# VectorE instead of GpSimd in the first network's weight decode and in the attention of blocks 1 to 8

## The chip, the cores and the metric

The kernel runs on one core of a Trainium2 chip. Its engines work side by side, each through its own queue in order: PE (TensorE, matmuls; PEld is its weight loads), DVE (VectorE), ACT (ScalarE), POOL (GpSimd) and SP (SyncE, which here issues most DMAs). The metric is the time of one execution on the device, in microseconds (us).

## The reference

Attention without a product of q and k, then two networks on its result:

```python
q_s = exp(q - max(q, axis=-1));  q_s /= sum(q_s, axis=-1) + 1e-09
k_s = exp(k - max(k, axis=2));   k_s /= sum(k_s, axis=2) + 1e-09   # along the sequence
x = einsum(q_s, einsum(k_s, v))                                    # 4608 tokens x 512
x = relu(x @ w_in) ** 2 @ w_out                                    # 512 -> 2048 -> 512
xn = x / sqrt(mean(x * x) + 1e-06) * rms_g
out = (silu(xn @ w_gate) * (xn @ w_val)) @ w_out2                  # 512 -> 1536 -> 512
```

q, k and v are 8 batches of 8 heads of 576 positions of 64 numbers. All is fp32.

## The kernel before

The tokens are worked off in 9 blocks of 512. For each block j, attention gives x in four parts, one for each pair of heads (hp), and the first network makes h = x @ w_in in 16 column tiles c, squares relu(h) to g and adds g @ w_out into four PSUM banks (`acc`). Such a pair of steps (j, c) is a unit: `p1_A` makes g of unit c, `p1_B` adds it two units later. The result of a block goes to DRAM after four copies out of PSUM (`e`, two by DVE, two by ACT). The second network runs behind about 955 us, over the same blocks, and is not touched.

Every fp32 matmul is made of three passes (`mm3`, L98): each operand is split into a high part (a rounding copy by ACT) and a low part (the difference, by DVE in `split`, L78). So each g costs one ACT copy and one DVE subtraction, and so do qT, kvd (k^T v of a head pair) and x.

The weights come as 64-bit floats and are decoded on the chip, tile by tile. A tile of weights is a key: i0 to i15 are column tiles of w_in, o0 to o15 row tiles of w_out; the second network has its own keys. `tick` moves the decode on by one key: `d_load` (512 KB by SP into one of three `raw` buffers), `d_words` (s, the high word scaled, L216, POOL; n, the low word, L224, ACT), `d_float` (three steps on DVE, L235, L243 and L247, that put the float together in one of two `t` buffers), `d_split` (high part by ACT, L251, low part by POOL, L252). The first network's keys are decoded while block 0 uses them, until about 140 us; to fill PE, h of block 1 is made along with them from i9 on. Keys of the second network are decoded from about 255 to 860 us, most of them in bursts up to 580 us (L295 makes sums of tiles on POOL, L252 splits them as `so`), and are written to DRAM.

Attention of block j + 1 goes along with block j's units. `A_STEPS` gives each head pair's steps with their unit: maxima of q and k (L471, L407, L410, DVE), subtraction of q's maxima (`a_qsub`, L477, POOL), `a_ktr` (PE transposes k's maxima, DVE reduces them, mc, L421, and spreads them, mcb, L423), `a_kb` (PE transposes them back into the PSUM tile `ps_kb`; ACT copies that to `mb`, L434), exp of q (ACT), `a_ksub` (two pieces, L445, POOL), the sum over q (`a_qsum`, L485 to L487, DVE), exp of k (`a_kexp`, ACT), scaling of q (`a_qn`, L494, POOL), k^T v (PE, normalized by DVE, L542 to L546), transposition of q (PE), x (PE). All PSUM tiles of attention (ps_kt, ps_kb, ps_kv, ps_q, ps_x) take turns in two buffers. Block 0's attention runs ahead of everything, with k's maxima subtracted straight from PSUM by DVE and q scaled by DVE.

The order on each engine is set by a scheduler, except for what `held` keeps in program order: such an instruction stays behind all that was written before it on its engine.

## Time and profile before

| | |
|---|---|
| time, median of 3 runs | 1826.89 us (1826.87 to 1830.08) |
| the profiled execution's own time | 1822.36 us |
| its span in the trace | 1820.6 us |
| PE busy | 1751.3 us (96%) |
| DVE busy | 1062.1 us (58%) |
| ACT busy | 750.9 us (41%) |
| POOL busy | 351.9 us (19%) |

POOL's share is a mean over the whole span; behind 860 us POOL does nothing. PE is near fully busy everywhere else than in the first 140 us and in some places between 280 and 560 us. So the stretches are to be read apart, by the windows view, and in each of them what PE waits for.

### The profile page before, as it was taken

To read this page: it belongs to the slowest core of one execution; us is meant where nothing else is said; L and a number is where in the kernel's file an instruction comes from. 1 tells how busy PE (TensorE), PEld (TensorE's weight loads), DVE (VectorE), ACT (ScalarE), POOL (GpSimd) and SP (SyncE) were. 2 spreads that over 40 slices of the span, in tenths; PEclk is the share of its full clock that TensorE was granted. 3 is DMA by queue.
4 is the path that set the end of the run, shared out by engine and by line. 5 is a ranking of instruction groups with operands and counts; after the bars stand their busy time and mean duration, and the time that the engine had idled before them with its cause. 6 is when DMAs were issued, how large, how long until landed. Compare 5 with 4: busy or idle time off the path is not lost.

```text
span 1820.6 us, 27274 instructions
## 1 busy us (share of the span) xinstructions
PE 1751.3 (96%) x10346; PEld 1520.1 (83%) x10346; DVE 1062.1 (58%) x1792; ACT 750.9 (41%) x1371; POOL 351.9 (19%) x349
## 2 busy tenths in 40 slices
PE   5789998999988999999999999999999999999998
PEld 3568886888767888888889999999999999999997
DVE  7875467374674534322245757676767675757544
ACT  4455435454554444444444232333333333333322
POOL 4666226154664412120000000000000000000000
PEclk9899999999989999999999999999999999999999
DMA  6787657688996755565757676767676767676673
GB/s 176 226 262 269 210 190 257 203 270 270 330 320 229 233 177 190 173 224 180 292 190 251 226 258 211 261 212 256 215 259 215 257 210 258 215 244 231 212 236 131
DMA packets 173634, 420.19 MB, mean 231 GB/s; under 512 B 57408, under 2 KB 74816, under 8 KB 172352
## 3 DMA queue, kind: packets, MB, share of 16 engines
q1 hardware_dynamic: 162272, 377.55, 63.4%
q10 hardware_dynamic: 11232, 40.90, 5.9%
q8 instruction: 83, 1.36, 0.3%
q14 instruction: 47, 0.39, 0.1%
HBM read 358.62 MB, written 59.77 MB: 230 GB/s over the span
## 4 chain that ended last, share of the span: by engine, by line
PE 75%; DMA 4%; DVE 2%; POOL 2%; issue 1%; ACT 1%; POOLq 0%; ACTq 0%; SPq 0%; DVEq 0%
PE acc L98 30%; PE ps_h L98 14%; PE ps_y L738 8%; PE ps_x L738 8%; PE ps_v L738 8%; PE ps_w L738 4%; DMA wd_s<-so 1%; DMA wd_a<-so 1%; POOL so L252 1%; PE ps_x L98 1%; PE ps_kv L526 1%; DMA wd_u<-so 1%; DVE t L243 1%; DVE t L235 0%; PE ps_q L508 0%
## 5 line engine op out<-in xcount | busy, mean ns | idle before, releaser
L98 PE MATMUL ps_h<-x,ws 128*128 128x512 f32 x1296 | 325.0, 401 | 6.7 <-POOL ws L252 5.9
L78 DVE TENSOR_TENSOR g<-r,g 128x512 fp32r<-128x512 f32 x252 | 191.3, 761 | 232.7 <-ACT g L77 230.7
L98 PE MATMUL acc<-g,ws 128*128 128x512 f32 x1296 | 315.8, 392 | 11.2 <-DVE e L620 5.6
L98 PEld LDWEIGHTS acc<-g,ws 128*128 128x128 f32 x1296 | 243.8, 189 | 64.6 <-POOL ws L252 7.3
L98 PEld LDWEIGHTS ps_h<-x,ws 128*128 128x128 f32 x1296 | 242.4, 192 | 59.3 <-POOL ws L252 7.9
L98 PE MATMUL acc<-ws,g 128*128 128x512 f32 x1080 | 265.7, 392 | 0.4 <-DVE g L78 0.4
L98 PEld LDWEIGHTS acc<-ws,g 128*128 128x128 f32 x1080 | 195.8, 189 | 37.9 <-DVE g L78 1.8
L77 ACT ACTIVATE g<-r 128x512 fp32r<-128x512 f32 x252 | 157.6, 626 | 44.5 <-DVE r L722 30.9
L720 ACT ACTIVATE sg<-c 128x256 f32<-128x256 f32 x108 | 56.5, 524 | 273.0 <-DVE c L753 223.0
L589 ACT ACTIVATE r<-ps_h 128x512 f32<-128x512 f32 x144 | 85.5, 594 | 202.7 <-PE ps_h L98 194.4
L738 PE MATMUL ps_x<-x,ws 128*128 128x256 f32 x972 | 129.5, 283 | 0.0
L738 PEld LDWEIGHTS ps_x<-x,ws 128*128 128x128 f32 x972 | 124.7, 191 | 3.0
L738 PE MATMUL ps_v<-x,ws 128*128 128x256 f32 x864 | 115.1, 283 | 0.0
L738 PEld LDWEIGHTS ps_v<-x,ws 128*128 128x128 f32 x864 | 111.0, 191 | 2.8
L98 PE MATMUL ps_h<-x,w 128*128 128x512 f32 x432 | 110.2, 405 | 0.0
L98 PE MATMUL acc<-g,w 128*128 128x512 f32 x432 | 108.1, 399 | 1.8 <-POOL w L252 1.5
L738 PE MATMUL ps_y<-x,ws 128*128 128x256 f32 x756 | 101.7, 284 | 0.0
L98 PEld LDWEIGHTS acc<-g,w 128*128 128x128 f32 x432 | 82.7, 193 | 19.8 <-POOL w L252 1.9
L753 DVE TENSOR_TENSOR c<-ps_v,u 128x512 f32<-128x512 f32 x54 | 37.4, 692 | 105.1 <-PE ps_v L738 105.1
L738 PEld LDWEIGHTS ps_y<-x,ws 128*128 128x128 f32 x756 | 95.1, 192 | 2.3 <-DVE sa L661 2.3
L98 PEld LDWEIGHTS ps_h<-x,w 128*128 128x128 f32 x432 | 81.7, 194 | 17.5
L590 ACT ACTIVATE r<-r 128x512 f32<-128x512 f32 x144 | 89.9, 628 | 3.0
(114 smaller groups left out, 2490.5 us busy)
## 6 DMA issues: line engine op xcount, KB each, us to landing
ws<-wd_s SPq DMA_DIRECT2D x135, 512.0 KB, 4.3
ws<-wd_a SPq DMA_DIRECT2D x117, 512.0 KB, 4.5
ws<-wd_o SPq DMA_DIRECT2D x96, 512.0 KB, 4.1
ws<-wd_i SPq DMA_DIRECT2D x90, 512.0 KB, 4.2
ws<-wd_u SPq DMA_DIRECT2D x90, 512.0 KB, 4.2
raw<-in_w_out SPq DMA_DIRECT2D x28, 512.0 KB, 4.9
raw<-in_w_gv SPq DMA_DIRECT2D x24, 512.0 KB, 6.1
wd_s<-so ACTq DMA_DIRECT2D x24, 512.0 KB, 5.5
```

Of the source, the lines that this page charges most:

```text
L77: held(j, nc.scalar.activation(out=dst[:, 0], in_=src, func=AF.Copy))
L78: nc.vector.tensor_tensor(out=dst[:, 1], in0=src, in1=dst[:, 0].bitcast(F32), op=ALU.subtract)
L98: ins = nc.tensor.matmul(ps, lhsT(a), rhs(b), start=first and n == 0, stop=last and n == 2)
L243: nc.vector.scalar_tensor_tensor(out=t, in0=sb, scalar=0x80000000, in1=t, op0=ALU.bitwise_and, op1=ALU.bitwise_or)
L252: eng.tensor_tensor(out=t[:, 1], in0=f, in1=t[:, 0].bitcast(F32), op=ALU.subtract)
L526: ins = nc.tensor.matmul(ps[h * D : (h + 1) * D, 0 : D + 1], ke[0:m, c, h, :], vt[0:m, c, h, :], start=c == 0, stop=c == SF,)
L589: nc.scalar.activation(out=r, in_=ps, func=AF.Relu)
L590: nc.scalar.activation(out=r, in_=r, func=AF.Square)
L720: nc.scalar.activation(out=r, in_=h[:, :, 0], func=AF.Sigmoid)
L738: nc.tensor.matmul(ps[:, g * HF : (g + 1) * HF], w[:, wa, (2 * g + kk) * P : (2 * g + kk + 1) * P], x[:, xa, kk, :], start=first and g == ...
L753: nc.vector.tensor_tensor(out=sv(name), in0=in0, in1=in1, op=ALU.add)
```

## The change

Four things change. The scaled high word s of the first network's keys is made by DVE for keys i and by ACT for keys o (the second network's stays on POOL), and the low parts of all 32 of these keys by DVE. k's maxima stay in the PSUM tile `ps_kb`: ACT's copy `mb` is gone, and DVE subtracts from PSUM, in the same step as the transposition (`a_kbs`, one unit earlier); exp of k is one unit earlier too. q's subtraction and scaling are DVE's in all blocks from 1 on. And the subtractions, the sum over q and the scaling are no longer held in program order. POOL keeps a memset of vt's column of ones and the second network's decode.

```diff
--- before.py
+++ after.py
@@ -213,14 +213,14 @@
         r = raws.pop(key).bitcast(U32).rearrange("p (n two) -> p n two", two=2)
         s = pools["d"].tile([P, 512], F32, tag="s", name="s", bufs=2)
         n = pools["d"].tile([P, 512], I32, tag="n", name="n", bufs=2)
-        nc.gpsimd.tensor_scalar(
-            out=s,
-            in0=r[:, :, 1].bitcast(F32),
-            scalar1=2.0**-112,
-            scalar2=0.0,
-            op0=ALU.mult,
-            op1=ALU.add,
-        )
+        hi = r[:, :, 1].bitcast(F32)
+        if key[0] == "o":
+            nc.scalar.activation(out=s, in_=hi, func=AF.Copy, scale=2.0**-112)
+        else:
+            eng = nc.vector if key[0] == "i" else nc.gpsimd
+            eng.tensor_scalar(
+                out=s, in0=hi, scalar1=2.0**-112, scalar2=0.0, op0=ALU.mult, op1=ALU.add
+            )
         nc.scalar.activation(out=n, in_=r[:, :, 0], func=AF.Copy, scale=2.0**-29)
         words[key] = s, n
 
@@ -265,7 +265,7 @@
 
     def d_split(key):
         t = slot_tile(key) if key in res1 else ring_tile()
-        w_split(t, floats.pop(key), nc.gpsimd)
+        w_split(t, floats.pop(key), nc.vector)
         if key not in res1:
             send(key, t, 2)
         wt[key] = t
@@ -428,27 +428,25 @@
             return
         ps = a_ps(j, hp, "ps_kb")
         held(j, nc.tensor.transpose(ps[:, 0:P], mcs.pop((j, hp)), ident))
-        mb = ps
-        if j > 0:
-            mb = pools["a"].tile([P, P], F32, tag="mb", name="mb", bufs=1)
-            nc.scalar.activation(out=mb, in_=ps[:, 0:P], func=AF.Copy)
-        mcs[j, hp] = mb
+        mcs[j, hp] = ps
 
     def a_ksub(j, hp):
         if j >= B:
             return
         kt = kts[j, hp]
         mx = mcs.pop((j, hp))[:, 0:P].rearrange("p (h d) -> p h d", h=2).unsqueeze(2)
-        eng = nc.gpsimd if j > 0 else nc.vector
         for rows, cs in k_parts:
             n = cs.stop - cs.start
-            ins = eng.tensor_tensor(
+            nc.vector.tensor_tensor(
                 out=kt[rows, :, cs, :],
                 in0=kt[rows, :, cs, :],
                 in1=mx[rows].to_broadcast([rows.stop, 2, n, D]),
                 op=ALU.subtract,
             )
-            held(j, ins)
+
+    def a_kbs(j, hp):
+        a_kb(j, hp)
+        a_ksub(j, hp)
 
     k_parts = ((slice(0, P), slice(0, SF)), (slice(0, SR), slice(SF, SF + 1)))
 
@@ -474,7 +472,8 @@
     def a_qsub(j, hp):
         qv = q_heads(j, hp)
         qm = qms.pop((j, hp)).unsqueeze(2).to_broadcast([P, 2 * NG, D])
-        held(j, nc.gpsimd.tensor_tensor(out=qv, in0=qv, in1=qm, op=ALU.subtract))
+        eng = nc.vector if j > 0 else nc.gpsimd
+        eng.tensor_tensor(out=qv, in0=qv, in1=qm, op=ALU.subtract)
 
     def a_qexp(j, hp):
         qv = q_heads(j, hp)
@@ -482,7 +481,7 @@
 
     def a_qsum(j, hp):
         qs = pools["a"].tile([P, 2 * NG], F32, tag="qs", name="qs")
-        held(j, nc.vector.reduce_sum(out=qs, in_=q_heads(j, hp), axis=AX.X))
+        nc.vector.reduce_sum(out=qs, in_=q_heads(j, hp), axis=AX.X)
         nc.vector.tensor_scalar_add(out=qs, in0=qs, scalar1=1e-9)
         nc.vector.reciprocal(out=qs, in_=qs)
         qms[j, hp] = qs
@@ -491,13 +490,12 @@
         qt = qts.pop((j, hp))
         rs = qms.pop((j, hp)).rearrange("p (h c) -> p h c", h=2).unsqueeze(3)
         qn = pools["a"].tile([P, NG, 2, D], F32, tag="qn", name="qn", bufs=2)
-        ins = (nc.gpsimd if j > 0 else nc.vector).tensor_tensor(
+        nc.vector.tensor_tensor(
             out=qn.rearrange("p c h d -> p h c d"),
             in0=qt,
             in1=rs.to_broadcast([P, 2, NG, D]),
             op=ALU.mult,
         )
-        held(j, ins)
         qns[j, hp] = qn
 
     def a_qT(j, hp):
@@ -830,7 +828,7 @@
 
 
     A_STEPS = ((-3, a_loadk), (-2, a_loadq), (0, a_qmax), (0, a_kmax), (1, a_qsub), (1, a_ktr))
-    A_STEPS += ((2, a_kb), (2, a_qexp), (3, a_ksub), (3, a_qsum), (3, a_loadv), (4, a_kexp))
+    A_STEPS += ((2, a_kbs), (2, a_qexp), (3, a_qsum), (3, a_loadv), (3, a_kexp))
     A_STEPS += ((4, a_qn), (5, a_kvn), (6, a_qT), (7, a_x))
     A_STARTS = {1: (-6, -4, -2, 0), 2: (-6, -3, 0, 3)}
     todo = {}
```

DVE behind block 0's x, in block 1's attention (t and s are buffers of the decode, w_649 is key i1's tile, g the first split of h). Before:

```order
L471 TENSOR_REDUCE qm<-qt 128x8
L487 RECIPROCAL qs<-qs 128x8
L423 COPY mcb<-mc 128x128
L78 TENSOR_TENSOR g<-r,g 128x512
L247 ISA t<-t,n 128x1024
L542 TENSOR_SCALAR rk<-ps_kv 128x1
L235 TENSOR_SCALAR t<-s 128x512
L543 RECIPROCAL rk<-rk 128x1
L243 SCALAR_TENSOR_TENSOR t<-s,t 128x512
L546 SCALAR_TENSOR_TENSOR kvf<-ps_kv,rk,mask 128x128
L247 ISA t<-t,n 128x1024
```

Now:

```order
L541 RECIPROCAL rk<-rk 128x1
L485 TENSOR_SCALAR qs<-qs 128x8
L410 TENSOR_TENSOR mk<-mk,kt 64x128
L544 SCALAR_TENSOR_TENSOR kvf<-ps_kv,rk,mask 128x128
L486 RECIPROCAL qs<-qs 128x8
L421 TENSOR_REDUCE mc<-ps_kt 128x1
L476 TENSOR_TENSOR qt<-qt,qm 128x512
L78 TENSOR_TENSOR kvd_0_87<-kvf,kvd_0_87 128x128
L423 COPY mcb<-mc 128x128
L78 TENSOR_TENSOR g<-r,g 128x512
L252 TENSOR_TENSOR w_649<-t,w_649 128x512
```

The low part of i1 was POOL's; it now stands on DVE behind the attention of block 1's first head pairs.

DVE in the later part of the first decode, about two keys (ws are weight tiles). Before:

```order
L78 TENSOR_TENSOR qT<-ps_q,qT 128x512
L243 SCALAR_TENSOR_TENSOR t<-s,t 128x512
L247 ISA t<-t,n 128x1024
L542 TENSOR_SCALAR rk<-ps_kv 128x1
L235 TENSOR_SCALAR t<-s 128x512
L543 RECIPROCAL rk<-rk 128x1
L243 SCALAR_TENSOR_TENSOR t<-s,t 128x512
L546 SCALAR_TENSOR_TENSOR kvf<-ps_kv,rk,mask 128x128
L78 TENSOR_TENSOR g<-r,g 128x512
L247 ISA t<-t,n 128x1024
```

Now:

```order
L252 TENSOR_TENSOR ws<-t,ws 128x512
L235 TENSOR_SCALAR t<-s 128x512
L221 TENSOR_SCALAR s<-raw 128x512
L243 SCALAR_TENSOR_TENSOR t<-s,t 128x512
L235 TENSOR_SCALAR t<-s 128x512
L247 ISA t<-t,n 128x1024
L243 SCALAR_TENSOR_TENSOR t<-s,t 128x512
L493 TENSOR_TENSOR qn<-qt,qs 128x2x4x64
L252 TENSOR_TENSOR ws<-t,ws 128x512
L247 ISA t<-t,n 128x1024
L235 TENSOR_SCALAR t<-s 128x512
```

The scaling s and the low parts ws have come in between the steps of the floats, and so has the scaling of q.

DVE at the end of block 1, from the g split to the first of its two e copies. Before:

```order
L78 TENSOR_TENSOR g<-r,g 128x512
L235 TENSOR_SCALAR t_3665<-s 128x512
L243 SCALAR_TENSOR_TENSOR t_3665<-s,t_3665 128x512
L247 ISA t_3665<-t_3665,n 128x1024
L235 TENSOR_SCALAR t_3745<-s 128x512
L243 SCALAR_TENSOR_TENSOR t_3745<-s,t_3745 128x512
L235 TENSOR_SCALAR t_3882<-s 128x512
L620 COPY e<-acc_2111 128x512
```

Now:

```order
L440 TENSOR_TENSOR kt<-kt,ps_kb 128x2x256
L78 TENSOR_TENSOR g<-r,g 128x512
L440 TENSOR_TENSOR kt<-kt,ps_kb 64x2x64
L484 TENSOR_REDUCE qs<-qt 128x8
L235 TENSOR_SCALAR t_3642<-s 128x512
L485 TENSOR_SCALAR qs<-qs 128x8
L235 TENSOR_SCALAR t_3719<-s 128x512
L486 RECIPROCAL qs<-qs 128x8
L243 SCALAR_TENSOR_TENSOR t_3642<-s,t_3642 128x512
L493 TENSOR_TENSOR qn<-qt,qs 128x2x4x64
L618 COPY e<-acc_2099 128x512
```

The subtraction of k's maxima, the sum over q and the scaling of q stand here now, and fewer steps of the decode.

DVE in the units around 513 us, up to the reduction mc. Before:

```order
L487 RECIPROCAL qs<-qs 128x8
L247 ISA t_6068<-t_6068,n 128x1024
L235 TENSOR_SCALAR t_6198<-s 128x512
L243 SCALAR_TENSOR_TENSOR t_6198<-s,t_6198 128x512
L78 TENSOR_TENSOR g<-r,g 128x512
L247 ISA t_6198<-t_6198,n 128x1024
L421 TENSOR_REDUCE mc<-ps_kt 128x1
L423 COPY mcb<-mc 128x128
```

Now:

```order
L247 ISA t_6025<-t_6025,n 128x1024
L235 TENSOR_SCALAR t_6152<-s 128x512
L243 SCALAR_TENSOR_TENSOR t_6152<-s,t_6152 128x512
L407 TENSOR_REDUCE mk<-kt 128x128
L78 TENSOR_TENSOR g<-r,g 128x512
L421 TENSOR_REDUCE mc<-ps_kt 128x1
L410 TENSOR_TENSOR mk<-mk,kt 64x128
L423 COPY mcb<-mc 128x128
```

The reduction mc, which frees a PSUM buffer, moved from behind the last step of a key to the place right behind the g split.

## Rows read from the trace of the kernel before

**Rows 1.** Windows by stage: each engine busy (instructions), PEclk, DMA share, GB/s.

```profile
36.50:140.00 103.50, 82.21 (x386) 60.49 (x385) 84.50 (x137) 53.66 (x105) 65.09 (x60) 0.91 0.70 224
...
250.00:580.00 330.00, 309.02 (x1560) 250.15 (x1559) 208.45 (x326) 165.28 (x310) 172.32 (x159) 0.96 0.81 269
580.00:955.00 375.00, 375.00 (x1824) 308.89 (x1823) 131.18 (x230) 165.28 (x290) 56.93 (x58) 1.00 0.61 205
```

**Rows 2.** PE's waits, 36.5 to 140 us: total, times, longest.

```profile
PE ps_h L98 <- POOL ws L252: 5.9, 4, 2.1
```

**Rows 3.** DVE's groups, 36.5 to 140 us: shapes, count, busy, mean ns, idle.

```profile
L243 DVE SCALAR_TENSOR_TENSOR t<-s,t 128x512 uint32<-128x512 uint32 x20 | 19.9, 995 | 0.5
L247 DVE CUSTOM_DVE_ANT_0 t<-t,n 128x1024 uint16<-128x1024 uint16 x21 | 17.2, 817 | 1.2
L235 DVE TENSOR_SCALAR t<-s 128x512 uint32<-128x512 uint32 x20 | 11.1, 553 | 13.2 <-POOL ws L252 10.5 <-POOL w L252 2.4 <-POOL s L216 0.3
...
L78 DVE TENSOR_TENSOR kvd<-kvf,kvd 128x128 fp32r<-128x128 f32 x5 | 5.2, 1033 | 0.1
...
L423 DVE COPY mcb<-mc 128x128 f32<-128x128 f32 x4 | 2.4, 611 | 0.0
```

**Rows 4.** DVE's timeline around 101 us: start, duration.

```profile
101.39 0.43 DVE L235 TENSOR_SCALAR t<-s 128x512 uint32<-128x512 uint32 x1 [1.56 <-POOL ws L252]
101.85 0.69 DVE L243 SCALAR_TENSOR_TENSOR t<-s,t 128x512 uint32<-128x512 uint32 x1
102.69 0.69 DVE L247 CUSTOM_DVE_ANT_0 t<-t,n 128x1024 uint16<-128x1024 uint16 x1
```

**Rows 5.** DVE's groups up to 36.5 us (block 0's attention).

```profile
L494 DVE TENSOR_TENSOR qn<-qt,qs 128x512 f32<-128x512 f32 x4 | 2.8, 701 | 1.2 <-PE ps_q L508 1.2
...
L445 DVE TENSOR_TENSOR kt<-kt,ps_kb 128x512 f32<-128x512 f32 x4 | 2.7, 674 | 0.0
...
L78 DVE TENSOR_TENSOR kvd<-kvf,kvd 128x128 fp32r<-128x128 f32 x3 | 0.8, 279 | 0.0
```

**Rows 6.** DVE's groups from 250 to 580 us.

```profile
L78 DVE TENSOR_TENSOR g<-r,g 128x512 fp32r<-128x512 f32 x50 | 48.0, 964 | 49.1 <-ACT g L77 49.1
L247 DVE CUSTOM_DVE_ANT_0 t<-t,n 128x1024 uint16<-128x1024 uint16 x34 | 33.9, 1006 | 1.2 <-ACT n L224 0.3
L243 DVE SCALAR_TENSOR_TENSOR t<-s,t 128x512 uint32<-128x512 uint32 x34 | 31.8, 939 | 0.6
L235 DVE TENSOR_SCALAR t<-s 128x512 uint32<-128x512 uint32 x34 | 22.8, 679 | 14.6 <-POOL so L252 12.6 <-POOL s L216 1.9
```

**Rows 7.** POOL's groups from 250 to 580 us.

```profile
L445 POOL TENSOR_TENSOR kt<-kt,mb 128x512 f32<-128x512 f32 x12 | 18.0, 1497 | 2.5 <-ACT mb L434 2.5
L494 POOL TENSOR_TENSOR qn<-qt,qs 128x512 f32<-128x512 f32 x12 | 14.2, 1183 | 47.1 <-DVE qs L487 47.1
L477 POOL TENSOR_TENSOR qt<-qt,qm 128x512 f32<-128x512 f32 x12 | 12.5, 1043 | 9.4 <-DMA kt<-in_k 4.8 <-DVE qm L471 4.6
```

**Rows 8.** PE's waits from 250 to 580 us.

```profile
PE ps_x L98 <- DVE qT L78: 6.3, 3, 2.9
PE acc L98 <- DVE e L620: 5.6, 1, 5.6
PE ps_kv L526 <- issue: 5.3, 1, 5.3
```

**Rows 9.** DVE's timeline around 280 and 513 us.

```profile
276.26 1.76 DVE L78 TENSOR_TENSOR g<-r,g 128x512 fp32r<-128x512 f32 x1
...
285.41 0.68 DVE L620 COPY e<-acc 128x512 f32<-128x512 f32 x1
...
512.67 0.86 DVE L235 TENSOR_SCALAR t<-s 128x512 uint32<-128x512 uint32 x1 [3.19 <-POOL so L252]
```

**Rows 10.** DVE's g splits from 860 to 955 us (POOL silent).

```profile
L78 DVE TENSOR_TENSOR g<-r,g 128x512 fp32r<-128x512 f32 x17 | 11.8, 692 | 47.2 <-ACT g L77 47.2
```

## The prediction

> **What bounds the kernel now.** I read the busy time by stage first. Between 36.5 and 140 us, the decode of the first network's weights, PE is busy for 82.2 of 103.5 us; between 250 and 580 us, the decode of the second network's, for 309.0 of 330; from 580 to 955 us it never stands still [rows 1]. The second network, behind 955 us, the change does not touch. So only two stretches can pay: 21.3 us of idle PE in the first and 21.0 us in the second. Each also has matmuls at a clock under full: granted 0.91 and 0.96 on average [rows 1].
>
> In the first stretch, PE's waits name one thing: the low half of a weight tile from POOL (L252). The row shown is one of three like it, 13.0 us together [rows 2]. DVE's groups tell why POOL is late: L235, the first step of a key's decode on DVE, sat idle for 13.2 us because its buffer was still being read by POOL [rows 3]. It is a loop: three steps on DVE, one on ACT, one on POOL, then DVE again. PE is a follower there.
>
> In the second stretch the waits that end PE's gaps point at DVE: an e copy 5.6 us, qT 6.3 us, and 5.3 us at ps_kv [rows 8]; that last one is booked as issue, but PE starts again right behind DVE's mc step, which frees a PSUM buffer, so I take it as DVE's too. DVE is 63% busy there on average (208.5 of 330, rows 1), and much more in bursts.
>
> **The change, part by part.** The first decode (36.5 to 140 us). POOL leaves the loop; the question is what DVE then needs for the same work. DVE was busy 84.5 us [rows 1]. Part of that is stretching beside POOL. Alone, L235 takes 0.43, L243 0.69, L247 0.69 [rows 4] and kvd 0.28 [rows 5]; in the stretch they take 0.553, 0.995, 0.817 and 1.033 [rows 3]. The small copy mcb takes 0.611 [rows 3] and stands for three kinds of small steps that are stretched; alone it is 0.21 (a row not shown). With POOL silent, 20 x 0.305 + 21 x 0.127 + 20 x 0.123 + 4 x 0.40 + 5 x 0.754 = 16.6 us go, and 67.9 are left.
>
> Then the additions. Scaling s for the 10 of 20 keys that begin with i: no row shows it on DVE; the nearest is L235, the same kind and shape, so 10 x 0.43 = 4.3. The low halves: 20 on DVE; the nearest row is a split of the same shape and type, 0.692 [rows 10], so 13.8. Attention for four head pairs: subtracting k's maxima, 0.674 from PSUM [rows 5] and 0.267 for the small second piece (its row is not shown), and q's subtraction and scaling, 0.701 each [rows 5], so 4 x 2.34 = 9.4. Together 27.5. The groups of [rows 3] and those not shown add to 91.9 us where the window counts 84.5, because neighbours overlap: 0.054 us for each of 137 instructions. For the 46 new ones that is 2.5 us back. 67.9 + 27.5 - 2.5 = 92.9 us.
>
> So DVE alone cannot finish in less than 92.9 us what took 103.5: at most 10.6 us to gain. It will not be fully busy. Of its 19.0 us of idle time, the 13.2 in front of L235 go [rows 3], the other 5.8 (for PE, for ACT) I keep. 98.7 us, a gain of 4.8. New on DVE is a wait inside a key: L252 needs ACT's high half. The order mostly puts the next key's steps between, so I add nothing; where L252 stands directly behind its key's L247, about half a microsecond is at stake. One place is worse: the low half of key i1 now stands behind block 1's whole first burst of attention, so PE has only key i0 and attention until then. The count above contains that burst, because the stretch is bounded by DVE's sum and PE has 21 us of slack. The ends: -10.6, and +3 if 3 us of round trips of that burst and of L252 appear on top of a DVE that gets none of its stretching back in the steps that pull most (kvd and mcb, 5.4 us). I take -4.8, near the middle.
>
> ACT gains ten scalings of keys o, about 0.66 each by its like-shaped step n, and loses four copies of maxima; it was busy for 53.7 of 103.5 us [rows 1], its idle time covers it. Loads: the same bytes in 98.7 instead of 103.5 us are 235 instead of 224 GB/s, and the second decode moved 269 [rows 1]. Both at nothing.
>
> The second decode (250 to 580 us). POOL keeps this network's decode and loses attention: 18.0 + 14.2 + 12.5 = 44.7 of its 172.3 us [rows 7, 1]. DVE gets 12 head pairs x 2.34 = 28.1 us. What it gets back: L247, L243, L235 and g take 1.006, 0.939, 0.679 and 0.964 here [rows 6], against 0.69, 0.69, 0.43 [rows 4] and 0.692 [rows 10]; that is 34 x 0.316 + 34 x 0.249 + 34 x 0.249 + 50 x 0.272 = 41.3 us of stretching beside 172.3 us of POOL, 0.24 each. For 44.7 us: 10.7. Net +17.4, DVE at 226 of 330, 68%.
>
> PE does not pay an average but its gaps, so I go through those with the order. The gap at 280 us (5.6): the e copy starts at 285.41, 7.4 us behind the end of the g split that started at 276.26 [rows 9]; in the new order only 3.5 us of DVE work stand between them, with 0.67 more ahead of the split: 3 us earlier at best. I take 2, since two of the steps between wait for POOL's s. The gap at 513 us (5.3): DVE sat 3.19 us until 512.67 for a POOL split [rows 9] that stood behind one scaling and one subtraction of q; these leave POOL and cost DVE 1.4 itself. Also mc now directly follows the g split. I take 2. The gap at 461 us (2.6 of the 6.3 for qT) has the same DVE rows ahead of it in both orders, decode alone: nothing. The gap at 555 us has more rows ahead, and fewer by POOL beside them: nothing. Against this, 12 new portions of 2.34 us, of which I let one show: +2. Sum -2. The ends: -10 (PE's three waits of rows 8 are 17.2 us; little over half goes) and +11.7 (five portions show).
>
> Blocks behind 580 us: PE has no gap there and DVE is busy 131 of 375 us [rows 1]; four head pairs are 9.4 us per block of about 94. k's maxima now hold a PSUM buffer until DVE has subtracted, not until ACT has copied; the buffer is wanted again two units later. The earlier kexp and the missing holds move work that PE does not wait for. Nothing, with 2 us either way.
>
> **Sum.** -4.8 - 2 = -6.8. The profiled execution took 1822.36 us and would take 1815.6. The median of the three runs, 1826.89, lies 4.5 us above it; I carry the same difference over: **1820 us**.
>
> **Rivals.** First, DVE too late in the second decode, **slower**. Place: the queue of DVE from 250 to 580 us, where ksub, both halves of it, two sums and a scaling now stand between g splits in the same units as the decode. A g split of the same shape costs 0.964 there against 0.692 alone, so 24 new subtractions and scalings with both inputs in SBUF would add 24 x 0.27 = 6.5 us to the 17.4. It decides where PE reaches ps_q, ps_x or a g tile before DVE has worked off a portion: if that is so for half of 12 head pairs, 6 x 2.34 = 14 us, less the 4.8: +9, about 1836. For it: DVE releases nearly all of PE's waits here. Against it: the average of 68%, and the two gaps above that shrink.
> The Trainium skill, "SBUF — State Buffer", section "Who interferes with whom", says that VectorE and GpSimd share a port pair as an exclusive lock, which an instruction of VectorE with two SBUF inputs also needs against a GpSimd instruction that reads SBUF. By that rule the 24 are exposed and the subtraction of k's maxima from PSUM is not; the trace agrees as far as L243, with two SBUF inputs, goes (0.995 beside POOL, 0.69 alone).
>
> Second, **no change**: DVE, now the bound of the first decode, idles 10 us and not 5.8 (the burst ahead of i1's low half, L252 behind ACT), and the second decode gives nothing back: 0 to -3, about 1825.
>
> Third, **a larger gain**: the first decode comes near DVE's sum (-9) and the second loses half of the two gaps that I only shortened by 2, with the slow clock behind them (-7): -16, about 1811.
>
> **Chances.** Forecast (-3.7 to -12) 0.48, larger gain 0.12, no change 0.18, slower 0.22. 0.2% is 3.65 us, about what a measurement of this kernel can tell from no change. Faster 0.60, same 0.18, slower 0.22. The range 1809 to 1834 leaves out some 0.06 below and 0.12 above; it spans -18 to +7, that is the low ends of both terms nearly together, and the slower case without its tail.
>
> **What would show it.** Right: between 36.5 and about 135 us DVE busy over 90%, POOL nearly empty, L243 near 0.69 us, PE's last wait for a weight tile some 5 us earlier, and its waits there on DVE L252; around 280 and 513 us shorter gaps. Wrong: DVE with over 10 us of idle time in the first stretch; new waits of PE for DVE between 290 and 580 us that sum to over 5 us; any gap of PE behind 580 us.

## The result

The changed kernel takes 1809.26 us, median of 4 runs (1806.02 to 1810.44); the kernel before, beside it, 1828.49 (1826.87 to 1835.79). The ratio is 0.9884, with a 95% interval of 0.9854 to 0.9915. The profiled execution of after took 1806.02 us with a span of 1804.2, against 1822.36 and 1820.6.

So it became faster by 19 us, in the medians, and by 16.4 in the two traces; 6.8 had been forecast. The time lies at the very lower end of the range, and it is the rival "a larger gain" (-9 and -7, to which 0.12 was given) that came true.

The stages of after, by the windows view (columns as in [rows 1]):

```profile
36.50:140.00 103.50, 89.82 (x434) 68.40 (x434) 97.65 (x205) 66.07 (x124) 0.60 (x4) 0.92 0.77 246
250.00:580.00 330.00, 312.67 (x1590) 254.08 (x1589) 219.68 (x379) 168.49 (x309) 121.80 (x110) 0.97 0.81 270
580.00:955.00 375.00, 375.00 (x1850) 310.08 (x1849) 141.39 (x259) 164.13 (x281) 18.81 (x19) 1.00 0.63 212
```

Against [rows 1]: between 36.5 and 140 us POOL has gone from 65.1 us to 0.6, DVE from 84.5 to 97.7, PE from 82.2 to 89.8. Between 250 and 580 us PE has 312.7 instead of 309.0 us of work done, at a clock of 0.97 instead of 0.96, with POOL at 121.8 instead of 172.3. Behind 580 us PE is as full as it was. (The first decode does not end at 140 us, as the description of the kernel before has it: its last low half ends at 184.8 us, with the change at 171.0. What ends by 140 us are PE's waits for it.)

How PE's waits changed in the first decode, and how DVE's groups did (36.5 to 126.5 us, where the same 20 keys are through; to be read against [rows 2, 3]):

```profile
PE ps_kb L430 <- DVE mcb L423: 4.9, 4, 2.7
PE ps_kt L419 <- DVE mk L410: 2.9, 2, 2.2
...
PE ps_h L98 <- DVE ws L252: 1.2, 2, 0.9
```

```profile
L247 DVE CUSTOM_DVE_ANT_0 t<-t,n 128x1024 uint16<-128x1024 uint16 x20 | 13.5, 678 | 0.1
L243 DVE SCALAR_TENSOR_TENSOR t<-s,t 128x512 uint32<-128x512 uint32 x20 | 13.4, 677 | 0.0
L252 DVE TENSOR_TENSOR ws<-t,ws 128x512 fp32r<-128x512 f32 x15 | 10.1, 674 | 1.5 <-ACT ws L251 1.5
L235 DVE TENSOR_SCALAR t<-s 128x512 uint32<-128x512 uint32 x20 | 8.1, 412 | 0.0
...
L78 DVE TENSOR_TENSOR g<-r,g 128x512 fp32r<-128x512 f32 x9 | 6.1, 674 | 0.0
...
L78 DVE TENSOR_TENSOR kvd<-kvf,kvd 128x128 fp32r<-128x128 f32 x5 | 1.4, 279 | 1.3 <-ACT kvd L77 1.3
...
L423 DVE COPY mcb<-mc 128x128 f32<-128x128 f32 x4 | 0.8, 203 | 0.0
```

L243 is back at 0.677 us (0.995 before), kvd at 0.279 (1.033), mcb at 0.203 (0.611). L235 no longer waits at all (13.2 us before). PE's waits for POOL are gone; its largest waits are for the maxima of block 1's attention, between 41 and 54 us.

A measure that goes through the whole study: the start of DVE's first e copy at the end of a block, which needs all matmuls of that block. "Between" is the time from block 0's to block 4's.

| kernel | block 0 | block 4 | between | median of the runs |
|---|---|---|---|---|
| before | 195.2 | 596.6 | 401.4 | 1826.9 to 1828.8 in five measurements |
| changed | 184.2 | 579.1 | 394.9 | 1809.3 |
| changed, once more | 184.1 | 578.0 | 393.9 | 1809.0 |
| decode alone (e1) | 185.6 | 590.8 | 405.2 | 1818.0 |
| attention alone (e2) | 192.9 | 582.9 | 390.0 | 1816.1 |
| POOL's attention from block 3 (e3) | 185.4 | 593.4 | 408.0 | 1821.8 |
| POOL's q from block 3 (e20) | 184.5 | 585.1 | 400.6 | 1813.7 |
| holds back (e4) | 186.8 | 584.3 | 397.5 | 1815.4 |
| ACT's copy of the maxima back (e10) | 187.0 | 585.1 | 398.1 | 1815.8 |
| five so buffers (e11) | 183.9 | 587.5 | 403.6 | 1815.8 |
| extra work on DVE (e5) | 185.6 | 575.0 | 389.4 | 1808.1 |
| extra work on POOL (e6) | 196.1 | 589.7 | 393.6 | 1819.3 |
| all s on ACT (e7) | 183.1 | 581.8 | 398.7 | 1808.7 |
| i1 on POOL (e8) | 181.7 | 580.6 | 398.9 | 1808.6 |
| block 2's maxima held (e16) | 182.3 | 574.5 | 392.2 | 1804.0 |
| the same, once more | 182.6 | 584.0 | 401.4 | 1807.6 |
| held, and i1 on POOL (e19) | 178.5 | 575.9 | 397.4 | 1804.2 |
| before, three t buffers (e9) | 195.1 | 604.7 | 409.6 | 1830.8 |

The two pairs of repeats say how such a table is to be read: block 0's end repeats to 0.3 us, the time between to no better than 1 us in one pair and 9 us in the other. So the first column tells of a single edit, the third only with the medians beside it. Nor do the columns add up to the medians: behind block 4's e copy the traces still differ by 5.6 us (1224.0 to 1229.6).

What varies between the blocks can be read from the windows view over just that stretch, here for the kernel before, the changed kernel, and the two executions with block 2's maxima held:

```profile
195.20:596.60 401.40, 380.42 (x1939) 308.98 (x1938) 238.09 (x382) 196.39 (x369) 183.72 (x174) 0.97 0.76 251
```

```profile
184.20:579.10 394.90, 377.57 (x1938) 307.48 (x1937) 252.74 (x446) 193.53 (x353) 123.88 (x114) 0.98 0.77 255
```

```profile
182.30:574.50 392.20, 375.06 (x1939) 304.75 (x1938) 258.17 (x450) 193.83 (x354) 124.83 (x114) 0.99 0.77 258
```

```profile
182.60:584.00 401.40, 380.35 (x1939) 309.33 (x1938) 257.95 (x449) 194.21 (x354) 125.21 (x114) 0.97 0.76 251
```

PE works off the same matmuls each time. The last two differ by 9.2 us: 3.9 are idle time of PE (17.1 against 21.1), and 5.3 are the same matmuls taking longer, at a granted clock of 0.97 instead of 0.99.

### The profile page after: what moved, and what is told of

Its sections match the earlier page's. It is cut to its first block, busy times and chain, and to the rows that moved or that the text cites. A ratio compares the mean times of both kernels' runs of the same rounds, so it can differ in the third digit from the quotient of the medians.

```text
span 1804.2 us, 27227 instructions
## 1 busy us (share of the span) xinstructions
PE 1746.3 (97%) x10346; PEld 1518.4 (84%) x10346; DVE 1100.0 (61%) x1960; ACT 754.6 (42%) x1359; POOL 154.6 (9%) x165
## 4 chain that ended last, share of the span: by engine, by line
PE 83%; DVE 8%; DMA 5%; issue 1%; ACT 1%; POOL 1%; SPq 0%; POOLq 0%; DVEq 0%; ACTq 0%
PE acc L98 33%; PE ps_h L98 18%; PE ps_y L736 8%; PE ps_x L736 8%; PE ps_v L736 8%; PE ps_w L736 4%; DMA wd_s<-so 2%; DVE t L243 1%; PE ps_x L98 1%; DVE t L247 1%; DMA wd_a<-so 1%; PE ps_kv L524 1%; DVE t L235 1%; PE ps_q L506 1%; DVE g L78 1%
## 5 line engine op out<-in xcount | busy, mean ns | idle before, releaser
L78 DVE TENSOR_TENSOR g<-r,g 128x512 fp32r<-128x512 f32 x252 | 182.8, 726 | 212.6 <-ACT g L77 210.3
```

Source lines behind the costliest of these rows:

```text
L78: nc.vector.tensor_tensor(out=dst[:, 1], in0=src, in1=dst[:, 0].bitcast(F32), op=ALU.subtract)
```

## The experiments

**The two halves apart.** One kernel with the decode's part of the diff alone, one with the attention's part alone.

```diff
 # e1_decode_only: the kernel before, d_words and d_split as in the change
 # e2_attention_only: the changed kernel, d_words and d_split as before
```

> The kernel before with one part of the change: the first network's decode off POOL (s by DVE for keys i and by ACT for keys o, all low parts by DVE); attention stays on POOL, with its holds. Theory A (the gain of the first decode comes from taking POOL out of the decode's loop, DVE is then the bound; the gain of the second decode comes from the attention's move): the first e copy of block 0 starts 8 to 10 us earlier than in the kernel before (195.2 us there, 184.2 with the whole change), nothing changes between block 0 and block 4, in all 8 to 10 us less. Theory B (POOL was late because attention stood in its queue; the decode alone would have been quick enough there): block 0 gains 3 us or less.

> The kernel with the whole change but the decode, which stays on POOL as before: only attention is moved. Theory A: the loop over POOL stays, L235 still waits for L252, and block 0's first e copy comes 3 to 5 us earlier at most (about 191 us); between block 0's and block 4's e copies 6 us are gained as with the whole change; in all 9 to 11 us less. Theory B: block 0 gains 8 to 11 us here already, in all 14 to 17 us less.

Measured: decode alone 1818.04 us, ratio 0.9945 (0.9927 to 0.9963); attention alone 1816.14, ratio 0.9933 (0.9908 to 0.9957). Theory A stands for the places: the decode's part gives 9.6 of the 11 us at block 0's end, the attention's part 2.3, and of what comes behind block 0 the attention's part gives all. By the medians, both beside the same runs of the kernel before, the parts are 9.8 and 11.7 us; together they gave 18 to 19 in other measurements, somewhat less than their sum. What was too small is the attention's part behind block 0: 9 us by the medians, where 2 had been put down, and 11.4 in the trace of e2, where 6 had been expected.

**Two buffers, or POOL's work?** L235 waited 13.2 us for a buffer [rows 3]. A third one takes that wait away and moves no work.

```diff
-            t = pools["d"].tile([P, 512], U32, tag="t", name="t", bufs=2)
+            t = pools["d"].tile([P, 512], U32, tag="t", name="t", bufs=3)   # in the kernel before
```

> The kernel before with three t buffers instead of two, nothing else: L235 no longer waits for POOL's split two keys back (13.2 us from 36.5 to 140 us). Theory A (it is POOL's work and its stretching of DVE that made the first decode long): PE's waits for POOL stay, block 0's first e copy (195.2) gains 3 us or less. Rival (the kernel before was bound by the latency of the loop through two buffers): it gains 6 us or more, as much of the change's 11 us without moving any work.

Measured: 1830.8 us, ratio 1.0009 (1.0000 to 1.0018); block 0 ends at 195.1, where it did. DVE's groups of this kernel from 36.5 to 140 us:

```profile
L243 DVE SCALAR_TENSOR_TENSOR t<-s,t 128x512 uint32<-128x512 uint32 x20 | 23.3, 1167 | 0.3
L235 DVE TENSOR_SCALAR t<-s 128x512 uint32<-128x512 uint32 x21 | 18.8, 896 | 7.2 <-POOL s L216 3.2 <-POOL w L252 2.8 <-POOL ws L252 1.2
L247 DVE CUSTOM_DVE_ANT_0 t<-t,n 128x1024 uint16<-128x1024 uint16 x21 | 17.9, 856 | 0.3
L78 DVE TENSOR_TENSOR g<-r,g 128x512 fp32r<-128x512 f32 x10 | 9.7, 968 | 0.0
```

The wait turned into stretching: L235 idles 7.2 instead of 13.2 us before it, but takes 0.896 instead of 0.553 us each, L243 1.167 instead of 0.995. DVE is busy for 93.9 us, 9.4 more, with nearly the same work. So the buffer alone was not the limit. That POOL beside DVE was, the next run shows.

**What POOL's work costs DVE.** Into the changed kernel comes one POOL instruction for each of the 32 keys, and nothing else.

```diff
+        if key[0] in ("i", "o"):
+            z = pools["d"].tile([P, 512], F32, tag="z", name="z", bufs=1)
+            nc.gpsimd.tensor_tensor(out=z, in0=s, in1=s, op=ALU.subtract)
         words[key] = s, n
```

> The changed kernel with one more instruction of POOL for each of the first network's 32 keys: a subtraction of two inputs in SBUF, 128 x 512, into a buffer that nobody reads, like the ones that the change took from POOL. No instruction is added on DVE. Theory A (DVE's instructions are stretched while POOL works, 0.26 us for each us of POOL in the first decode of the kernel before): some 18 x 1.2 us of POOL before the last split that PE waits for stretch DVE by 5 to 6 us, and block 0's first e copy comes that much later than 184.2; L243 there goes from 0.68 to about 0.8 us. Rival (DVE was long because it waited within its instructions for data, not because POOL worked): nothing changes but POOL's busy time.

Measured: 1819.3 us, ratio 0.9957 (0.9944 to 0.9971), and block 0 ends at 196.1: 11.9 us later than with the change, all that the change had won there. POOL and DVE in it, from 36.5 us to 140 and to 126.5:

```profile
L227 POOL TENSOR_TENSOR z<-s 128x512 f32<-128x512 f32 x22 | 32.4, 1472 | 56.7 <-DVE s L221 43.0 <-ACT s L218 10.6 <-DVE rk L544 2.7
```

```profile
L250 DVE CUSTOM_DVE_ANT_0 t<-t,n 128x1024 uint16<-128x1024 uint16 x17 | 14.2, 843 | 0.0
L246 DVE SCALAR_TENSOR_TENSOR t<-s,t 128x512 uint32<-128x512 uint32 x17 | 11.4, 680 | 0.0
L238 DVE TENSOR_SCALAR t<-s 128x512 uint32<-128x512 uint32 x18 | 10.7, 604 | 0.0
...
L78 DVE TENSOR_TENSOR g<-r,g 128x512 fp32r<-128x512 f32 x8 | 6.9, 860 | 0.0
```

The mechanism is shown, and its size was twice what I expected. L243 (L246 here) hardly pays up to 126.5 us, 0.680; up to 140 us it takes 0.754 on average. Those that happen to meet POOL's pay: L235 (L238) 0.604 for 0.412, L247 (L250) 0.843, g 0.860. 17 keys got through instead of 20 by 126.5 us. The added instruction also reads s, and could have held DVE up by keeping s's buffer; but no wait of DVE for POOL stands in this trace from 36.5 to 140 us.

A mean hides how the stretching comes about. In the kernel before, 17 of the 20 L243 from 36.5 to 140 us took 0.69 us like those with POOL silent; three took 1.42, 3.09 and 3.66, and these three make the mean of 0.995. The longest, on DVE, and what POOL did meanwhile:

```profile
63.69 3.66 DVE L243 SCALAR_TENSOR_TENSOR t<-s,t 128x512 uint32<-128x512 uint32 x1
```

```profile
63.93 1.03 POOL L477 TENSOR_TENSOR qt<-qt,qm 128x512 f32<-128x512 f32 x1
64.94 0.63 POOL L216 TENSOR_SCALAR s<-raw 128x512 f32<-128x512 f32 x1
65.54 1.25 POOL L252 TENSOR_TENSOR ws<-t,ws 128x512 fp32r<-128x512 f32 x1
```

POOL's run ends at 66.79 us, DVE's instruction 0.56 us later. So a few instructions wait for whole instructions of POOL, and which ones do depends on the order.

**DVE's sum as the bound.** An instruction more on DVE for each key (s scaled once more into an unread buffer), or one less for each key i (its s on ACT).

```diff
+            nc.vector.tensor_scalar(out=z, in0=s, scalar1=2.0**-112, scalar2=0.0, op0=ALU.mult, op1=ALU.add)   # e5
-        if key[0] == "o":
+        if key[0] in ("i", "o"):                                                                              # e7
```

> The changed kernel with one more instruction of DVE for each of the first network's 32 keys: s scaled once more into a buffer that nobody reads. It takes 0.41 us and starts 0.34 us behind its neighbour. Theory A (DVE's sum bounds the first decode once POOL is out): of the 32, about 18 lie between block 0's x and the last split that PE waits for, so block 0's first e copy comes 18 x 0.34 = 6 us later than with the change (184.2 there). Rival (the loads, ACT or PE bound it): 2 us or less.

> The changed kernel with the scaled word s of all 32 keys of the first network on ACT, not of the o keys alone: DVE loses 9 instructions before the last split that PE waits for, ACT gains 9 of 0.67 us. Theory A (DVE's sum is the bound of the first decode): block 0's first e copy comes 9 x 0.34 = 3 us earlier than with the change (184.2). Rival (ACT is late with s, since its queue also holds the high halves and g): no gain or a loss there.

Measured: 1808.07 (ratio 0.9899, 0.9877 to 0.9921) and 1808.7 (0.9889, 0.9874 to 0.9904); block 0's end 1.4 us later, and 1.1 us earlier. Both are a fraction of what was expected. For e5 the order gives the reason: the scheduler put three subtractions and maxima of block 2's q and one of its k, which with the change stand ahead of the last split PE waits for, behind it, 5.3 us by their durations against 18 x 0.34 = 6.1 added. So e5 does not test what it was made for, and it showed that DVE's queue held work that nobody needed yet. For e7 the windows show PE busy for 25.4 of the 26.5 us from 100 to 126.5: DVE stopped being the bound when a little was taken from it, so PE was not far from being one with the change already.

**The work that nobody needed yet.** Block 2's maxima held in program order.

```diff
+        held(1 if j == 2 else 0, ins)   # in a_qmax (reduce_max of q) and a_kmax (tensor_reduce of k)
```

> The changed kernel with the maxima of block 2's q and k held in program order, so that the scheduler no longer places them (and the subtractions that follow) ahead of the first decode's splits: with the change, three head pairs' maxima and subtractions of q and two maxima of k of block 2 stand there on DVE, 6.6 us by their durations, 5.9 with the overlap. Theory A (DVE's sum is the bound): block 0's first e copy comes 3 to 6 us earlier than with the change (184.2). Rival (they only fill DVE's waits for PE and ACT, and cost nothing): within 1 us.

> The changed kernel with block 2's maxima held, once more. Theory A (DVE's sum bounds the first decode until these steps are out of it; block 2's steps cost nothing later): 3 to 6 us less than the changed kernel in the same call. Rival (the gain of the single look was the luck of the second decode's gaps): the same time within 2 us.

Block 0 ends at 182.3 and 182.6, 1.5 to 1.9 us earlier than with the change, below the 3 to 6 expected. The windows tell why, from 100 to 126.5 us, the changed kernel first, then this one:

```profile
36.50:60.00 23.50, 13.64 (x60) 9.24 (x60) 21.54 (x50) 9.16 (x18) 0.12 (x1) 0.71 0.44 118
...
100.00:126.50 26.50, 24.05 (x105) 18.26 (x104) 26.36 (x51) 18.20 (x35) 0.00 (x0) 1.00 0.91 309
```

```profile
36.50:60.00 23.50, 14.17 (x62) 9.42 (x60) 20.80 (x49) 9.48 (x20) 0.12 (x1) 0.71 0.46 122
...
100.00:126.50 26.50, 25.94 (x114) 20.10 (x114) 24.73 (x48) 20.15 (x38) 0.00 (x0) 1.00 0.97 331
```

With the change DVE is full (26.36 of 26.5) and PE waits; with the maxima held PE is full (25.94) and DVE is not. What PE then lacks lies ahead, from 36.5 to 60 us, where it works 14 of 23.5 us. In the whole: 1803.95 us (the changed kernel 1809.26, but not beside it), and 1807.56 beside 1809.0. The ranges of that pair overlap (1801.6 to 1812.2 and 1803.8 to 1816.1): not told apart.

**Key i1.** Its low half stands behind block 1's attention on DVE. It goes back to POOL, in the changed kernel and with the maxima held.

```diff
-        w_split(t, floats.pop(key), nc.vector)
+        w_split(t, floats.pop(key), nc.gpsimd if key == ("i", 1) else nc.vector)
```

> The changed kernel with the low half of one weight tile, key i1, back on POOL: with the change it stands on DVE behind block 1's first attention, and PE has 9.4 us of gaps between 40 and 54 us. Theory A (DVE's sum is the bound of this stretch, PE has the slack): the gap at 53 us goes, but block 0's first e copy moves by no more than the 0.6 us that DVE saves, up to 2 us with what the order changes. Rival (the late i1 is a loss of its own): PE gets its matmuls 10 us earlier, and block 0 ends 3 to 5 us earlier.

> Block 2's maxima held, and key i1's low half on POOL. With the maxima held, DVE was busy for 24.7 of the 26.5 us from 100 to 126.5 us and PE for 25.9: PE is the bound there, and its 10 us of gaps from 41 to 60 us are what is left. Theory A: now that DVE's sum is no longer the bound, an earlier i1 counts in full, and block 0's first e copy comes 3 to 6 us earlier than with the maxima held alone (182.3). Rival (DVE is still the bound, and i1 saves it 0.6 us): 1 us or less.

Block 0's end: 2.5 us earlier than with the change alone (between the two theories; DVE's own saving is 0.6), and 3.8 to 4.1 us earlier than with the maxima held, as expected where PE is the bound. 178.5 us is the earliest end of block 0 in the study, 16.7 us ahead of the kernel before. In the medians, 1808.55 and 1804.2 us (the latter beside 1809.0 for the changed kernel; 1801.8 to 1806.9 against 1803.8 to 1816.1): five less, with overlapping ranges. It may be the better version; the runs don't prove it.

**Which part of attention matters in the second decode.** POOL gets attention back from block 3 on, all of it or q's two steps; or ACT's copy comes back with the subtraction left on DVE.

```diff
+        mb = pools["a"].tile([P, P], F32, tag="mb", name="mb", bufs=1)      # e10 (all blocks from 1), e3 (j > 2)
+        nc.scalar.activation(out=mb, in_=ps[:, 0:P], func=AF.Copy)
-            nc.vector.tensor_tensor(                                        # a_ksub, e3
+            (nc.gpsimd if j > 2 else nc.vector).tensor_tensor(
-        eng = nc.vector if j > 0 else nc.gpsimd                             # a_qsub, and a_qn alike, e3 and e20
+        eng = nc.vector if 0 < j < 3 else nc.gpsimd
```

> The changed kernel, but for blocks 3 to 8 the maxima's copy by ACT is back and the subtractions and q's scaling are POOL's again (without holds, at the new steps); blocks 1 and 2 and the whole decode as changed. Theory A: block 0's end stays 11 us early, block 1's 14.6, and of the rest of the gain in the second decode (about 3 us from block 1's to block 4's end) most is lost: 13 to 15 us less than the kernel before. Rival: the gain in the second decode came from the order without holds and from the earlier kexp, not from POOL's silence: then it stays at 16 to 17 us.

> The changed kernel, but q's subtraction and scaling are POOL's again for blocks 3 to 8 (without holds); k's subtraction stays on DVE from PSUM. Between block 0's and block 4's first e copies the kernel with all of attention on DVE takes 394.9 us, with all of it on POOL from block 3 on 408.0. Theory A (the loss comes from POOL's queue: whatever of attention stands in it waits for the second network's splits and delays them, and PE waits behind): most of the loss is back, 403 us or more. Rival (it is k's subtraction alone, with the copy by ACT and the two pieces on POOL): 398 us or less.

> The changed kernel with ACT's copy of k's maxima back, so that the PSUM buffer is free without DVE; the subtraction stays on DVE, now from SBUF. With the change PE waits 6.1 us for DVE's subtraction at ps_q between 250 and 580 us (5.5 at 530 us). Theory A (a PSUM buffer that is held in DVE's queue is a new wait that the change brought): these two waits go, and block 4's end comes 4 to 8 us earlier than with the change (579.1). Rival (the wait only shows where the burst is late anyway, or ACT is late with the copy, being held up for the buffers of so): another wait takes its place, within 2 us of the changed kernel, or slower, since the subtraction now has two inputs in SBUF beside POOL.

Measured: 1821.79 (ratio 0.9964, 0.9952 to 0.9975), 1813.66 (0.9927, 0.9911 to 0.9942) and 1815.78 (0.9935, 0.9913 to 0.9956), against 1809 with the change. In e3 more was lost than expected, some 12.6 us by the medians (6.0 less than the kernel before, where 13 to 15 were expected), though block 0 still ended 9.8 us early. q's two steps cost about 4.6 of it by the medians: between the two expectations (400.6 us between the blocks). In the trace of e20, 1.3 us of the 5.7 between the blocks are more idle time of PE, and the rest is its matmuls at 0.97 of the clock instead of 0.98. And the copy by ACT alone costs some 6.6, against theory A: the two waits at ps_q did go, but others came, for qT 10.4 us and for e 3.9 from 195 to 600 us. Only e3's interval stands well clear of both of the changed kernel's (0.9854 to 0.9915 and 0.9887 to 0.9931); those of e20 and e10 overlap with the second, so their sizes are rough. From 250 to 580 us the subtraction takes 0.828 us when it reads the copy in SBUF (e10), and 0.677 from PSUM (changed kernel):

```profile
L444 DVE TENSOR_TENSOR kt<-kt,mb 128x512 f32<-128x512 f32 x12 | 9.9, 828 | 0.0
```

```profile
L78 DVE TENSOR_TENSOR g<-r,g 128x512 fp32r<-128x512 f32 x49 | 43.5, 887 | 36.8 <-ACT g L77 36.8
...
L476 DVE TENSOR_TENSOR qt<-qt,qm 128x512 f32<-128x512 f32 x13 | 10.0, 772 | 0.3
L493 DVE TENSOR_TENSOR qn<-qt,qs 128x512 f32<-128x512 f32 x13 | 9.9, 763 | 0.7 <-PE ps_q L506 0.5
...
L440 DVE TENSOR_TENSOR kt<-kt,ps_kb 128x512 f32<-128x512 f32 x13 | 8.8, 677 | 3.4 <-PE ps_kb L430 3.2
```

The means are to be split. Of e10's 12 subtractions 5 met an instruction of POOL and took 1.03 us on average, the others 0.681. Of the changed kernel's 13 only 4 met one, and these took 0.673 to 0.675, less than the rest. Of q's scalings and subtractions, with both inputs in SBUF, 4 of 13 each met one, and took 0.93 and 0.96 on average.

The rest of that loss is a guess: the copy stands in ACT's queue, which in the changed kernel waits 51 us for the writes of so to DRAM from 250 to 600 us (27 in the kernel before). No run took that wait away: the one that tried, with five so buffers, follows.

**Five so buffers.**

```diff
-            t = pools["q"].tile([P, 2, 512], F32R, tag="so", name="so", bufs=4)
+            t = pools["q"].tile([P, 2, 512], F32R, tag="so", name="so", bufs=5)   # and kvf with one buffer for two
```

> The changed kernel with five instead of four so buffers for the second network's split tiles (and one buffer fewer for kvf, to make room). From 250 to 600 us ACT waits 51 us for the writes of so to DRAM with the change, 27 in the kernel before, and holds up g and qT behind it. Theory A (what is left of PE's gaps from 495 to 561 us, some 11 us, is released by DVE and ACT, which are late because ACT stands before a full so): ACT's waits for so's writes go below 25 us and block 4's end comes 3 to 6 us earlier than 579.1. Rival (the writes are bound by the DMA engines, 0.9 busy there): one more buffer only shifts the wait, within 2 us.

Measured: 1815.79 us, ratio 0.9926 (0.9911 to 0.9941), slower than the change by the medians, with overlapping intervals. ACT still waits 46 us for these writes, and new gaps of PE came at 289, 300 and 434 us (4.5, 4.0 and 2.3), where it waited for DVE's subtraction of the maxima and for qT. The missing kvf buffer confounds it: the run tells nothing on so for certain.

**Holds back.**

```diff
+            held(j, ins)   # again in a_ksub, a_qsub, a_qsum and a_qn
```

> The changed kernel with the four holds back (both subtractions, the sum over q and the scaling keep program order); all engines as changed. Theory A: the holds hardly matter, within 3 us of the changed kernel, since DVE is bound by its sum. Rival C: the dropped holds are what lets DVE fill its waits for PE and ACT in block 1's burst and in the bursts of the second decode; then block 0's end is 3 to 6 us later than with the change, and the whole 5 to 10 us slower.

Measured: 1815.36 us, ratio 0.9934 (0.9910 to 0.9958). Rival C is nearer: block 0 ends 2.6 us later than with the change, the whole takes 6 us more by the medians (the intervals overlap by a little). In the prediction the dropped holds were put down at nothing.

**The changed kernel once more**, beside e16, e19 and e20:

> The changed kernel once more, beside the two versions that follow, so that they stand on the same chip: 1805 to 1811 us.

1809.0 us, ratio 0.9909 (0.9887 to 0.9931).

## Why the prediction was right in direction and too small

The mechanism held, and the steps that failed are sizes: in the first term DVE's sum with its idle time (98.7 us forecast, 90.0 measured), in the second the gaps (-2 forecast, -6.5 measured), with the clock left out of both and the missing holds put at nothing.

**What bounds the kernel: right.** PE's waits for POOL in the first decode are gone, DVE is the bound in their place (26.36 of 26.5 us busy from 100 to 126.5 us), and PE has no gap from 580 to 955 us. DVE is the bound by a small margin: e7 and e16 took some 3 and 6 us of work off it, and block 0's end came only 1.1 and 1.5 to 1.9 us earlier, with PE full.

**First term, -4.8, measured -11.0 at block 0's end.** The method, DVE's sum, was right; each of its three numbers was on the cautious side. Forecast for the same 20 keys: 92.9 us of DVE and 5.8 idle, 98.7. Measured up to 126.5 us: 86.2 and 3.8, 90.0. The difference is 8.7 us: (1) The busy times of after's groups add to 99.1 us where I had 102.8. I had left g, the small sums over q and the small maxima as stretched as they were, took 0.69 where 0.675 to 0.68 came, and counted one L247, one low half and one g more than fell into the stretch; three subtractions and a maximum of block 2's q, placed ahead, took 2.7 back. With smaller ones, 3.7 us in all. (2) Over 184 instructions 0.070 us each are saved by overlap (99.1 less 86.2, by 184), not 0.054, and I had reckoned with the smaller: 3.0 us. The overlap of a pair did not change. An instruction that follows at once on work that it needs nothing from starts 0.075 to 0.08 us ahead of its neighbour's end, on average 0.079 over 93 pairs before and 0.075 over 174 with the change, and 0.078 over the 47 of e6 that stand beside POOL's work; one that needs its neighbour's result does not [rows 4]. What changed is how many do. Such a pair, before, while POOL was at work:

```profile
44.27 1.02 DVE L486 TENSOR_SCALAR qs<-qs 128x8 f32<-128x8 f32 x1
45.20 0.67 DVE L471 TENSOR_REDUCE qm<-qt 128x8 f32<-128x512 f32 x1
```

(3) Idle 3.8 and not 5.8: 2.0 us. By DVE that is 13.5 us earlier. PE's last wait for a weight tile (key o8) ends 9.3 us earlier, because the window that I summed over ended 6.7 us behind that wait and now ends 2.5 behind it. And then the clock adds, which I had left out of both terms. PE's timeline there, before and after:

```profile
133.35 3.91 PE L98 MATMUL acc<-g,w 128*128 128x512 f32 x9 [1.45 <-POOL w L252]
137.08 1.09 PE L98 MATMUL ps_h<-x,ws 128*128 128x512 f32 x4
```

```profile
124.03 1.89 PE L98 MATMUL acc<-g,w 128*128 128x512 f32 x7 [0.61 <-DVE w L252]
125.75 1.52 PE L98 MATMUL ps_h<-x,ws 128*128 128x512 f32 x6
```

Nine matmuls behind the wait took 3.91 us, with TensorE's clock granted at 0.83 on average from 130 to 140 us (at 0.50, the lower of its two levels, from 133.7 to 137.1, right behind the wait of 1.45 us); now seven take 1.89, at 1.00 throughout. So the next key's matmuls start 11.3 us earlier. Even the end that I gave as DVE's bound, -10.6, was passed, since the sum under it was too large; and the value between the ends was taken "near the middle", by no row.

**i1 behind the burst: nearly right.** PE idles for 9.9 us from 36.5 to 60 us, where it idled for 5.7 before, and that cost little time while DVE was the bound: e8 gained 2.5 us at block 0's end, e19, with DVE relieved, 4.

**Second term, -2; measured -6.5 in this pair of traces, some -9 by the medians of e1 and e2.** (Behind block 4 the pair differs by +1.1: -11.0 - 6.5 + 1.1 = -16.4.) The gaps of PE, by their place in the kernel before:

| gap | before | changed | forecast |
|---|---|---|---|
| end of block 1 (286 us) | 5.6 | 2.4, and 0.6 at ps_q | -2 |
| 463 us, qT | 2.6 | 1.8 | 0 |
| 519 us, ps_kv | 5.3, and 0.8 ahead of it | 0.9 and 0.5 | -2 |
| 549 to 560 us, ps_q and qT | 5.4 | 1.3, then 5.5 at ps_q and 3.4 | 0 |
| all over 0.4 us, 185 to 600 us | 20.3 | 16.7 | -2 |

```profile
PE ps_q L506 <- DVE kt L440: 6.1, 2, 5.5
PE ps_x L98 <- ACT qT L77: 3.4, 1, 3.4
PE acc L98 <- DVE e L618: 2.4, 1, 2.4
```

(The waits are those from 195 to 600 us with the change.) The two gaps that I followed through the order shrank by 2.6 and 4.7 us, more than I took (3 us "at best", and 1.8 with the new place of mc besides, were worked out, and 2 and 2 taken). In the changed kernel the second is booked to mc, as I had taken it. A new one came, against which I had put only the 2 us of one portion that shows: ps_q waits 5.5 us for a PSUM buffer in which k's maxima are held until DVE has subtracted. "Wanted again two units later" was right, but DVE came later still there, behind a wait of 2.7 us for POOL and two L247 of 2.8 us together:

```profile
523.62 0.88 DVE L235 TENSOR_SCALAR t<-s 128x512 uint32<-128x512 uint32 x1 [2.72 <-POOL so L252]
...
526.21 2.80 DVE L247 CUSTOM_DVE_ANT_0 t<-t,n 128x1024 uint16<-128x1024 uint16 x2
```

Of the 6.5 us, 3.6 are less idle time of PE and 2.9 are the clock: the same matmuls took 380.4 us at 0.97 before and 377.6 at 0.98 with the change. I had put the clock into the third rival alone. And the missing holds, which I had put at nothing, are worth 2.6 us at block 0's end and some 3 more behind it by e4's medians. How much of the rest is less work of POOL beside DVE and how much the new order, no run tells apart.

**DVE's load in the second decode: too high.** 226 us of 330 was forecast, 219.7 measured (in a stretch that lies 11 to 17 us further on in the program, with two keys less and a head pair more). POOL lost more than the 44.7 us that I had: the small second piece of k's subtraction, 7.3 us there, was left out, and the window shows 50.5 less. The four kinds whose stretching I counted got back 10.2 us (10.7 forecast), and small ones that I had not counted 6 more, mcb above all (0.678 us before, 0.361 now). The 26 new steps on q there take 0.763 and 0.772 us beside POOL and 0.686 and 0.676 without, 2.3 us of stretching together, where the slower rival had put 6.5. The Trainium skill, "SBUF — State Buffer", section "Who interferes with whom", says that an instruction of VectorE with at most one input in SBUF does not contend with GpSimd, unless it runs in a mode that uses both port pairs: the subtraction from PSUM agrees, 0.673 to 0.675 where it met POOL's work, 0.679 with POOL silent. It also counts tensor_scalar among the instructions that can enter such a mode, and L235, with one input, is stretched indeed (0.604 in e6). L243, on which the prediction leaned, does agree, but its mean is a poor measure: it has two SBUF inputs in e6 as well, and took 0.680 up to 126.5 us and 0.754 up to 140; which instruction pays depends on what stands beside POOL's.

**The slower rival** did not come: PE's new waits for DVE are 5.5 and 0.6 us at ps_q. One of the prediction's signs of being wrong did show, new waits of over 5 us; it was a poor sign, since the gaps that went outweighed them. **No change** fell with DVE's idle time of 3.8 us. The larger gain was priced right (-9 and -7, by halves of gaps and the clock behind them) and given too small a chance; in part that is luck, for the two gaps lost 7.3 of 11.7 us and not half, and the new one took most of it back.

**Open.** The same kernel's second decode takes 392.2 us in one execution and 401.4 in another (e16): 3.9 us of that is idle time of PE and 5.3 the granted clock, but why PE's gaps and the clock differ between executions of one kernel is not settled. What ACT's copy costs beside the stretching (e10) isn't either.

## What to carry to other kernels

Where an engine is stretched by a neighbour, cost the move at the sum of undisturbed durations, less the overlap of every neighbour that needs nothing from the one before it, and look for idle time by whom it waits for, not as a share. Taking away a wait for a buffer without taking away the work behind it can turn the wait into longer instructions. Before adding work to an engine that becomes the bound, look in the order for what it does too early: holding block 2's maxima back won 1.5 to 1.9 us at block 0's end, taking nine scalings off DVE 1.1. And where many small gaps depend on each other, split a difference into PE's idle time and the granted clock before giving it a cause.

## What the runs showed of the hardware

POOL subtractions of 128 x 512 whose result nobody reads, 22 of them of 1.47 us from 36.5 to 140 us, made the first decode 12 us longer. The stretching falls on a few instructions: of 20 L243 from 36.5 to 140 us of the kernel before 17 took 0.69 us, and the longest, 3.66, ended 0.56 us behind a run of three POOL instructions. A subtraction on DVE that reads PSUM and SBUF was not stretched where it met POOL's work (4 of them, 0.673 to 0.675 us); the same with both inputs in SBUF was (5 of them, 1.03 on average). Neighbours on DVE that don't need each other overlapped by 0.075 to 0.08 us, whether POOL worked or not. And the same 1939 matmuls took 375.1 us in one execution and 380.4 in another, at a granted clock of 0.99 and 0.97.
